# One line moved in an expert loop: a tile's result ahead of the split of the next w2

## The chip, the cores and the metric

The program runs on one core of a Trainium2 chip. The metric is the device time of one execution in microseconds (us); a smaller time is better. TensorE (PE) multiplies matrices, VectorE (DVE), ScalarE (ACT) and GpSimd (POOL) work on elements, and SyncE (SP) issues most of the transfers. Each engine takes its own list of instructions in order, and semaphores order the engines among each other.

## The reference

Three layers follow one another. A chunked attention gives 4608 rows of 512 numbers. A layer of 8 experts follows: each row goes to one expert, the one with the largest logit. The last layer is a dense one with a swish.

```python
def _moe_ref(x, expert_emb, tau, w1, w2):
    ...
    expert_idx = np.argmax(logits, axis=1)
    ...
    for e in range(E):
        mask = expert_idx == e
        h = np.maximum(x[mask] @ w1[e], 0.0)
        out[mask] = gate_w[mask, None] * (h @ w2[e])

def _moe2_ref(x, w_in, w_out):
    h = x @ w_in
    g = h * (1.0 / (1.0 + np.exp(-1.702 * h)))
    return (g @ w_out).astype(np.float32)
```

In the expert layer w1 is 512 x 1024 and w2 is 1024 x 512 for each expert. The change lies in this layer.

## The kernel before, in words

The kernel has three stages. In the profiled execution attention and gating take the first 245 us, the expert stage runs to about 678 us, and the dense layer takes the rest. The order of the instructions on every engine is the order in which the code is written (`tc.manual_schedule()`).

**Tiles.** The rows are sorted by expert and cut into tiles of 128 rows of one expert; an expert with fewer rows left fills its last tile with others. Tiles 0 to 2 come before the loop; the loop of line 1354 takes tiles 3 to 38 (`NSURE` to `SURE - 1`).

**Two halves of a number.** Every float32 operand is held as two float16 parts, a high and a low one, and each product is three matmuls. Weights come from memory as float32 into a staging buffer (`stg` for w1, `stgB` for w2) and are split on the core by `w_split`: ScalarE writes the high part (line 793), VectorE the low part (line 798), in 4 pieces of 128 x 1024. The one copy on the core, `w1HL` and `w2HL`, is written over when the expert changes.

**A switch.** Which tile begins a new expert is known only at run time. `swap(i, which)` (line 843) therefore puts the split under `tc.If(flag[i] > 0)` (line 847), a branch that ScalarE and VectorE take or pass. Whoever uses the weight afterwards waits for both engines at this place, whether the branch was taken or passed. In the profiled execution the expert changes at tiles 8, 12, 19, 25, 28, 32 and 37. `load_next` then has SyncE issue the load of the expert after that into the staging buffer, under a branch of its own (line 837).

**A tile's work.** `mm1(i)` is the first product, 96 matmuls 128 x 128 (line 897) into PSUM; ScalarE (line 904) and VectorE (line 905) take it out as `hT`, the high and the low part. `mm2_part(i)` is the second product, 24 matmuls 128 x 512 (line 930), into a PSUM bank `py`, of which there are two. `mm2_evac(i)` is what this document calls the result of a tile: ScalarE sums the squares of a row (line 943), VectorE makes a scale of it in small steps (lines 944 to 953), ScalarE writes the scaled high part (`y`, line 956), VectorE the low part and a tail (lines 957 and 960), and SyncE stores `y` (line 968).

**One round of the loop.** Round i issues in this order, each engine seeing only its own part:

1. first product of tile i, its transfer out of PSUM (`hT`);
2. transfers for later tiles: the transposed rows of tile i + 2, and others;
3. `swap(i + 1, 1)`: the branch with the split of w1 for tile i + 1;
4. a step of `dec`: a piece of w_in or w_out of the last layer is converted (lines 1251 to 1258 on VectorE, 1154 and 1148 on ScalarE, the rest on GpSimd), in rounds 5 to 36, two steps in rounds 11 and 19;
5. second product of tile i - 1;
6. `swap(i, 2)`: the branch with the split of w2 for tile i;
7. the result of tile i - 1.

So on TensorE the products stand as first(i), second(i - 1), first(i + 1), second(i), and the second product of tile i is the first to use what step 6 of round i leaves in `w2HL`.

Of the kernel before, what the change touches and what calls it, by code (L numbers as in the profile page):

```python
# [34 lines left out]
def kernel(  # L35
# [732 lines left out]
    def reg(ap, engines, hi):  # L768
        return nc.values_load(ap, engines=engines, min_val=0, max_val=hi)
# [10 lines left out]
    def w_split(which, c, n, eng, st=stg):  # L780

        hlf, o = divmod(c * n, 2048)
        _, H_, L_ = WL[which]
        if which == 1 and n == 1024:
            k, f = slice(c % 2 * 2, c % 2 * 2 + 2), slice(c // 2 * 512, c // 2 * 512 + 512)
            H_, L_ = H_[:, k, f], L_[:, k, f]
            src = st[c % 2].rearrange("p (a f) -> p a f", a=2)[:, :, f]
        else:
            flat = slice(c * n, (c + 1) * n)
            H_ = H_.rearrange("p a f -> p (a f)")[:, flat]  # L790
            L_ = L_.rearrange("p a f -> p (a f)")[:, flat]
            src = st[hlf][:, o:o + n]
        nc.scalar.activation(out=H_, in_=src, func=AF.Copy, scale=2.0 ** W_EXP)
        if eng is nc.gpsimd:
            eng.tensor_tensor(out=src, in0=src, in1=w_pow.to_broadcast([128, n]), op=ALU.mult)
            eng.tensor_tensor(out=L_, in0=src, in1=H_, op=ALU.subtract)
        else:
            eng.scalar_tensor_tensor(
                out=L_, in0=src, scalar=2.0 ** W_EXP, in1=H_, op0=ALU.mult, op1=ALU.subtract
            )  # L800
# [29 lines left out]
    def load_next(i, which):  # L830

        if which == 1:
            nxt[i] = (
                reg(nf_i[0:1, i:i + 1], [ENG.SP], 1), reg(nx_i[0:1, i:i + 1], [ENG.SP], NE - 1)
            )
        fl, e = nxt[i]
        with tc.If(fl > 0):
            for hlf in range(2):
                w_load(e, which, hlf, stage[which])
# [3 lines left out]
    def swap(i, which):  # L843

        if which == 1:
            flag[i] = reg(fl_i[0:1, i:i + 1], [ENG.Activation, ENG.DVE], 1)
        with tc.If(flag[i] > 0):  # L847
            for c in range(4):
                w_split(which, c, 1024, nc.vector, stage[which])
        load_next(i, which)  # L850
# [18 lines left out]
    def fetch(i):  # L869
        xg = mo.tile([128, 2 * DM], F16, tag="xg", name="xg", bufs=2)  # L870
        src = xs[0:NPART * 128, :] if i < NSURE else xs[:, :]
        nc.gpsimd.indirect_dma_start(  # L872
            out=xg[:, :], out_offset=None, in_=src,
            in_offset=bass.IndirectOffsetOnAxis(ap=mt_t[i].bitcast(I32)[:, 1:2], axis=0),
        )
        xg_t[i] = xg

    def turn(i):
        xT = mo.tile([128, 2 * KD, 128], F16, tag="xTm", name="xTm", bufs=2)
        nc.sync.dma_start_transpose(xT, xg_t.pop(i))  # L880
        xTm_t[i] = xT
# [28 lines left out]
    def mm1(i):  # L910
        for q in range(4):
            mm1_part(i, q)
# [19 lines left out]
    def mm2_evac(i):  # L932
        hT_t.pop(i)
        p = py_t.pop(i)
        mt = mt_t.pop(i)
        y = mo.tile([128, YP], F16, tag="y", name="y", bufs=2)
        ysq = mo.tile([128, DM], F16, tag="ysq", name="ysq", bufs=1)
        s = mo.tile([128, 4], F32, tag="ys", name="ysc", bufs=2)
        si = s.bitcast(I32)
        c_i = mt.bitcast(I32)[:, 0:1]  # L940
        tail = y[:, 2 * DM:YP].bitcast(I32).rearrange("p (a two) -> p a two", two=2)
        n = (YP - 2 * DM) // 4
        nc.scalar.activation(out=ysq, in_=p, func=AF.Square, scale=2.0 ** -20, accum_out=s[:, 0:1])
        nc.vector.tensor_scalar(si[:, 3:4], c_i, EXP_BITS, None, op0=ALU.bitwise_and)
        nc.vector.tensor_copy(tail[:, :, 0], mt.bitcast(I32)[:, 1:2].to_broadcast([128, n]))
        nc.vector.tensor_scalar(s[:, 0:1], s[:, 0:1], Y_MIN * 2.0 ** -40, None, op0=ALU.max)
        nc.vector.tensor_scalar(
            si[:, 1:2], si[:, 0:1], 24, 23, op0=ALU.logical_shift_right, op1=ALU.logical_shift_left
        )
        nc.vector.tensor_scalar(  # L950
            si[:, 1:2], si[:, 1:2], -1.0, float((BIAS + Y_TOP - 20) << 23), op0=ALU.mult, op1=ALU.add
        )
        nc.vector.scalar_tensor_tensor(  # L953
            out=si[:, 2:3], in0=c_i, scalar=MAN_BITS, in1=si[:, 1:2], op0=ALU.bitwise_and, op1=ALU.bitwise_or
        )
        nc.scalar.activation(out=y[:, 0:DM], in_=p, func=AF.Copy, scale=s[:, 2:3])  # L956
        nc.vector.scalar_tensor_tensor(
            out=y[:, DM:2 * DM], in0=p, scalar=s[:, 2:3], in1=y[:, 0:DM], op0=ALU.mult, op1=ALU.subtract
        )
        nc.vector.scalar_tensor_tensor(  # L960
            out=tail[:, :, 1], in0=si[:, 3:4].to_broadcast([128, n]), scalar=float(BIAS << 23),
            in1=si[:, 1:2].to_broadcast([128, n]), op0=ALU.add, op1=ALU.subtract,
        )
        if i < NSURE:
            nc.sync.dma_start(out=ys[i * 128:(i + 1) * 128, :], in_=y)
        elif i < SURE:
            row = reg(idx_y[0:1, i:i + 1], [ENG.SP], NT)
            nc.sync.dma_start(out=ys[bass.ds(row, 128), :], in_=y)
        else:
            nc.gpsimd.indirect_dma_start(  # L970
                out=ys[:, :], out_offset=bass.IndirectOffsetOnAxis(ap=idx_y[:, i:i + 1], axis=0),
                in_=y[:, :], in_offset=None,
            )
# [161 lines left out]
    def big_load(b):  # L1135

        nc.sync.dma_start(
            out=raw_o[b % NRAW].rearrange("p f two -> p (f two)"),
            in_=block_of(b).rearrange("p f two -> p (f two)"),
        )  # L1140
# [213 lines left out]
    for i in range(NSURE, SURE):  # L1354
        mm1(i)
        if i + 2 < SURE:
            turn(i + 2)
        if i == NSURE:
            load_next(NSURE - 1, 2)
            for b in range(NRAW):  # L1360
                big_load(b)
        if i + 3 < SURE:
            fetch(i + 3)
        if i + 4 < SURE:
            find(i + 4)
        if i + 1 < SURE:
            swap(i + 1, 1)
        if NSURE + 2 <= i < LASTD:
            for _ in range(2 if i in (NSURE + 8, NSURE + 16) else 1):
                next(dec, None)  # L1370
        if i > NSURE:
            mm2_part(i - 1, 0, KF)
        if i == SURE - 1:
            scales_b(0)
            early = sums(0)
            for _ in range(2):
                next(early)
        swap(i, 2)
        if i > NSURE:
            mm2_evac(i - 1)  # L1380
        if i == SURE - 2:
            scales_a(0)
        if i == LASTD:
            next(dec, None)
            dec_stack.close()
            mlp = ctx.enter_context(tc.tile_pool(name="mlp", bufs=1))

            def prep(j):
                idc = mlp.tile([128, 4, 2], I32, tag="idc", name="idc", bufs=2)
                nc.sync.dma_start(  # L1390
                    out=idc,
                    in_=ys[j * 512:(j + 1) * 512, 2 * DM:2 * DM + 4].bitcast(I32).rearrange(
                        "(a p) c -> p a c", p=128
                    ),
                )
                yT = mlp.tile([128, 2 * KD, 512], F16, tag="yT", name="yT", bufs=1)
                for a in range(4):
                    nc.sync.dma_start_transpose(
                        yT[:, :, a * 128:(a + 1) * 128],
                        ys[j * 512 + a * 128:j * 512 + (a + 1) * 128, 0:2 * DM],  # L1400
                    )
                yT_t[j], id_t[j] = yT, idc

            ring = {}

            def load_w(j, n):
                ring[j, n] = mlp.tile([128, 2, KG * 128], F16, tag="ring", name="ring", bufs=NRING)
                o = PROD[n][0]
                nc.sync.dma_start(
                    out=ring[j, n], in_=wod[2 * o:2 * o + 2].rearrange("h p f -> p h f")  # L1410
                )

            op6 = mlp.tile([128, 4096], F16, name="op6")
            prep(0)
            for n in range(NRING):
                load_w(0, n)
# [316 lines left out]
```

## Time and profile before

| what | number |
|---|---|
| median of 3 runs | 1385.8 us (1385.78 to 1392.34) |
| profiled execution, its own time | 1381.04 us |
| its span, first to last instruction | 1379.3 us |
| mean granted clock of TensorE, as a share of full speed | 0.968 |
| busy over the span: PE | 1248.8 us (91%) |
| busy over the span: DVE | 1048.1 us (76%) |
| busy over the span: ACT | 723.7 us (52%) |
| low parts of w2 in the loop, DVE line 798 | 28 pieces, mean 1349 ns |

The profile is one execution, recorded on the core. Busy is the time in which an engine worked on an instruction; register, branch and semaphore instructions do not count. Matmuls overlap each other, so their ends are modelled. The rows of a timeline give the start, the duration, the engine, the source line, the operation, what is written and read, and in square brackets how long the engine was idle before and which work released it. A releaser written ACTq or DVEq is not an instruction that computes but the queue of that engine: there the branch of line 847.

### The profile page before, as it was taken

What the parts mean: (1) busy time and instruction counts of PE and PEld (TensorE: products, weight loads), DVE (VectorE), ACT (ScalarE), POOL (GpSimd) and SP (SyncE); (2) the same over time, 40 slices, a digit from 0 to 9 for tenths busy, and PEclk for the clock granted to TensorE, in tenths of its full rate; (3) what the DMA queues carried; (4) which work ended last, traced back from release to release, by engine and by line L of the source; (5) the groups of instructions that cost most, each with busy time, mean ns of one, the idle gap of its engine ahead of it and who ended that gap; (6) DMA issues with size and microseconds to landing.
All of it is one profiled execution on the core that took longest, in us unless ns stands there. A gap on an engine that the chain in (4) does not pass through costs nothing.

```text
span 1379.3 us, 35366 instructions
## 1 busy us (share of the span) xinstructions
PE 1248.8 (91%) x14098; PEld 1028.0 (75%) x14098; DVE 1048.1 (76%) x1897; ACT 723.7 (52%) x1288; POOL 737.6 (53%) x687
## 2 busy tenths in 40 slices
PE   6886666999899899899989999999999999999996
PEld 5665555676577576667678888888888888888885
DVE  3888788648887878886679696968787896969681
ACT  6986755235534445454454545545454645455452
POOL 1564544214533444453157575766767675757664
PEclk9998877999999999999999999999999999999998
DMA  9999986388675759986506253443526072634412
GB/s 202 232 182 185 172 161 155 99 225 238 192 179 164 204 143 270 277 240 161 154 3 192 84 154 123 123 153 85 192 33 223 22 205 71 157 120 123 153 62 92
DMA packets 225749, 213.97 MB, mean 155 GB/s; under 512 B 134104, under 2 KB 178648, under 8 KB 225568
## 3 DMA queue, kind: packets, MB, share of 16 engines
q1 hardware_dynamic: 211024, 184.51, 52.7%
q0 software_dynamic: 7152, 19.70, 4.4%
q10 hardware_dynamic: 7392, 7.36, 1.7%
q8 instruction: 112, 1.84, 0.6%
q14 instruction: 69, 0.57, 0.1%
HBM read 155.02 MB, written 36.85 MB: 139 GB/s over the span
## 4 chain that ended last, share of the span: by engine, by line
PE 33%; DVE 5%; issue 5%; ACT 4%; POOL 3%; POOLq 0%; ACTq 0%; DVEq 0%
PE pa L1441 8%; PE pd L1441 8%; PE pb L1441 8%; PE gb L1441 4%; PE pc L1441 4%; DVE zA L1296 3%; ACT zA L1465 1%; POOL w2HL L1303 1%; POOL out_dram L1588 1%; ACT stgB L1299 1%; ACT w1HL L1299 1%; DVE stgB L1296 0%; ACT hT L1583 0%; ACT op L1299 0%; DVE zC L1462 0%
## 5 line engine op out<-in xcount | busy, mean ns | idle before, releaser
L1441 PEld LDWEIGHTS <-wS 128*128 128x128 f16 x3024 | 296.5, 98 | 59.7 <-issue 21.6
L897 PEld LDWEIGHTS <-w1HL 128*128 128x128 f16 x3744 | 215.6, 99 | 21.9 <-ACTq L847 7.5
L897 PE MATMUL ph<-xTm,w1HL 128*128 128x128 f16 x3744 | 221.4, 221 | 9.7 <-ACTq L847 5.3
L930 PE MATMUL py<-w2HL,hT 128*128 128x512 f16 x936 | 214.8, 386 | 12.3 <-ACTq L847 3.8
L930 PEld LDWEIGHTS <-hT 128*128 128x128 f16 x936 | 91.3, 99 | 119.8 <-issue 22.1
L872 POOL DMA_INDIRECT xg<-xs,mt x39 | 40.1, 1029 | 148.0 <-DMA mt<-mtab 90.2
L1441 PEld LDWEIGHTS <-w2HL 128*128 128x128 f16 x864 | 84.5, 98 | 10.6
L1441 PEld LDWEIGHTS <-w1HL 128*128 128x128 f16 x864 | 84.6, 98 | 9.8
L956 ACT ACTIVATE y<-py,ysc 128x512 f16<-128x512 f32 x39 | 26.8, 687 | 114.5 <-DVE ysc L953 114.5
L416 POOL TENSOR_TENSOR x<-x,sx_all 128x512 f32<-128x512 f32 x33 | 34.2, 1037 | 98.0 <-DVE rd L386 46.3
L1296 DVE TENSOR_TENSOR zA<-zA 128x512 f32<-128x512 f32 x72 | 73.2, 1017 | 10.8 <-POOL w2HL L1303 9.5
L905 DVE SCALAR_TENSOR_TENSOR hT<-ph,hT 128x512 f16<-128x512 f32 x78 | 51.8, 685 | 32.2 <-ACT hT L904 32.2
L1465 ACT ACTIVATE zA<-zA 128x512 f32<-128x512 f32 x72 | 45.2, 629 | 57.8 <-DVE zA L1462 35.3
L1303 POOL TENSOR_TENSOR w1HL<-zA,w1HL 128x512 f16<-128x512 f32 x36 | 54.1, 1503 | 36.6 <-ACT w1HL L1299 36.6
L904 ACT ACTIVATE hT<-ph 128x512 f16<-128x512 f32 x78 | 44.8, 594 | 49.6 <-PE ph L897 49.5
L1149 POOL TENSOR_TENSOR wS<-d_f,wS 128x512 f16<-128x512 f32 x28 | 38.3, 1386 | 52.2 <-ACTq L847 27.5
L1441 PE MATMUL pd<-stg,wS 128*128 128x256 f16 x456 | 55.9, 276 | 3.5 <-ACT stgB L1299 3.5
L1588 POOL DMA_INDIRECT out_dram<-hT,idc x36 | 35.6, 988 | 35.6 <-ACT hT L1583 32.5
L311 ACT ACTIVATE kuT<-tp 64x512 f32<-64x512 f32 x72 | 45.1, 626 | 17.4 <-PE tp L306 16.4
L306 PE MATMUL tp<-identF,ku 128*128 128x128 f32 x144 | 25.8, 322 | 29.3 <-DMA ku<-in_k_dram 25.6
L1441 PE MATMUL pa<-stg,wS 128*128 128x256 f16 x432 | 51.6, 273 | 0.7 <-ACT stgB L1299 0.7
L340 DVE TENSOR_REDUCE mx<-sp 128x8 f32<-128x512 f32 x36 | 24.8, 688 | 35.7 <-PE sp L333 35.6
(370 smaller groups left out, 3151.2 us busy)
## 6 DMA issues: line engine op xcount, KB each, us to landing
ring<-wod SPq DMA_DIRECT2D x63, 1024.0 KB
stg<-in_moe_w_dram SPq DMA_DIRECT2D x14, 1024.0 KB
stgB<-in_moe_w_dram SPq DMA_DIRECT2D x14, 1024.0 KB
ys<-y SPq DMA_DIRECT2D x39, 258.0 KB
vt<-in_v_dram SPq DMA_DIRECT2D x64, 144.0 KB
xs<-xr SPq DMA_DIRECT2D x36, 256.0 KB
raw_o<-in_moe_w_in_dram SPq DMA_DIRECT2D x16, 512.0 KB
raw_o<-in_moe_w_out_dram SPq DMA_DIRECT2D x16, 512.0 KB
```

Of the source, the lines that this page charges most:

```text
L311: lambda r=r, p=p, dst=dst: nc.scalar.activation(out=dst[:, :, r], in_=p[r * 64:(r + 1) * 64], func=AF.Copy)
L872: nc.gpsimd.indirect_dma_start(out=xg[:, :], out_offset=None, in_=src, in_offset=bass.IndirectOffsetOnAxis(ap=mt_t[i].bitcast(I32)[:, 1:2] ...
L897: nc.tensor.matmul(p[:, f % 4], wt[:, c, fs], xT[:, a, :], start=(c == 0 and a == 0 and wt is w1H), stop=(c == KD - 1 and wt is w1L),)
L904: nc.scalar.activation(out=hi, in_=p, func=AF.Relu)
L905: nc.vector.scalar_tensor_tensor(out=lo, in0=p, scalar=0.0, in1=hi, op0=ALU.max, op1=ALU.subtract)
L930: nc.tensor.matmul(p, hT[:, a, :], wt[:, c, :], start=st, stop=sp)
L1149: nc.gpsimd.tensor_tensor(out=L_, in0=f, in1=H_, op=ALU.subtract)
L1296: nc.vector.tensor_tensor(out=o, in0=x, in1=p, op=op)
L1303: eng.tensor_tensor(out=lo, in0=x, in1=hi, op=ALU.subtract)
L1441: nc.tensor.matmul(dst, lhs(a, k, ab), rhs(b, k), start=first and ab == abs_[0] and k == 0 and m == 0, stop=(k == n - 1 and m == 2), skip_ ...
L1465: nc.scalar.activation(out=z, in_=z, func=AF.Sigmoid, scale=1.702 * 2.0 ** -G_EXP)
L1588: disjoint("out", nc.gpsimd.indirect_dma_start(out=out[:, :], out_offset=bass.IndirectOffsetOnAxis(ap=id_t[j][0][:, 2 * h + t, 0:1], axis= ...
```

## The change

The two statements of steps 6 and 7 change places: the result of tile i - 1 is now issued ahead of the branch with the split of w2 for tile i. Nothing else is different.

```diff
             early = sums(0)
             for _ in range(2):
                 next(early)
-        swap(i, 2)
         if i > NSURE:
             mm2_evac(i - 1)
+        swap(i, 2)
         if i == SURE - 2:
             scales_a(0)
```

**VectorE.** The rows are of one round of the loop. L847 is the branch, L798 are the pieces of w2 in it, L944 to L960 are the result, L905 is the next tile's `hT`. Before:

```order
L847 COMPARE_AND_BRANCH
L798 SCALAR_TENSOR_TENSOR w2HL<-stgB_4652,w2HL 128x1024 x2
L798 SCALAR_TENSOR_TENSOR w2HL<-stgB_4653,w2HL 128x1024 x2
L847 UNCONDITIONAL_BRANCH x2
L837 UNCONDITIONAL_BRANCH
L944 TENSOR_SCALAR ysc<-mt 128x1
L945 COPY y<-mt 128x2
L946 TENSOR_SCALAR ysc<-ysc 128x1
L947 TENSOR_SCALAR ysc<-ysc 128x1
L950 TENSOR_SCALAR ysc<-ysc 128x1
L953 SCALAR_TENSOR_TENSOR ysc<-mt,ysc 128x1
L957 SCALAR_TENSOR_TENSOR y<-py_5395,ysc,y 128x512
```

And now, from the last rows of the result on:

```order
L953 SCALAR_TENSOR_TENSOR ysc<-mt,ysc 128x1
L957 SCALAR_TENSOR_TENSOR y<-py_5395,ysc,y 128x512
L960 SCALAR_TENSOR_TENSOR y<-ysc 128x2
L847 COMPARE_AND_BRANCH
L798 SCALAR_TENSOR_TENSOR w2HL<-stgB_4652,w2HL 128x1024 x2
L798 SCALAR_TENSOR_TENSOR w2HL<-stgB_4653,w2HL 128x1024 x2
L847 UNCONDITIONAL_BRANCH x2
L837 UNCONDITIONAL_BRANCH
L905 SCALAR_TENSOR_TENSOR hT<-ph,hT 128x512 x2
```

The whole branch, taken or not, has moved from ahead of L944 to behind L960, in every round. ScalarE's list changes in the same way, with L793 for L798 and L943 and L956 for the result.

**SyncE.** The rows are of the end of one round and the start of the next. L837 is the branch with the loads of a later w2 (L775), L968 is the store of the result, L880 is the transpose of a later tile's rows. Before:

```order
L837 COMPARE_AND_BRANCH
L775 ISA
L775 DMA stgB_4652<-in_moe_w_dram 128x4x512
L775 ISA
L775 DMA stgB_4653<-in_moe_w_dram 128x4x512
L837 UNCONDITIONAL_BRANCH x2
L769 TENSOR_LOAD idx_y
L769 ISA x2
L968 ISA
L968 DMA ys<-y 128x1032
L880 DMA_TRANSPOSE xTm<-xg 128x8x128
```

And now:

```order
L769 TENSOR_LOAD idx_y
L769 ISA x2
L847 UNCONDITIONAL_BRANCH
L968 ISA
L968 DMA ys<-y 128x1032
L837 COMPARE_AND_BRANCH
L775 ISA
L775 DMA stgB_4652<-in_moe_w_dram 128x4x512
L775 ISA
L775 DMA stgB_4653<-in_moe_w_dram 128x4x512
L837 UNCONDITIONAL_BRANCH x2
L880 DMA_TRANSPOSE xTm<-xg 128x8x128
```

The store has moved ahead of the loads; the transpose stands behind both, as it did.

## Rows read from the trace of the kernel before

**Rows 1.** Windows: busy of each engine (x instructions), TensorE's granted clock, DMA share, GB/s; tiles 3 to 38.

```profile
278.70:678.50 399.80, 379.34 (x4133) 269.58 (x4131) 310.41 (x545) 190.30 (x324) 159.68 (x134) 0.98 0.75 207
```

**Rows 2.** Timeline of TensorE: second products of tiles 5 and 6, no switch near.

```profile
299.80 5.34 PE L930 MATMUL py<-w2HL,hT 128*128 128x512 f16 x24
...
310.33 5.34 PE L930 MATMUL py<-w2HL,hT 128*128 128x512 f16 x24
```

**Rows 3.** Timeline of VectorE: the last instruction of the result of tile 5.

```profile
308.11 0.15 DVE L960 SCALAR_TENSOR_TENSOR y<-ysc 128x2 int32<-128x2 int32 x1
```

**Rows 4.** Timeline of VectorE: last dec instruction of round 24, ahead of the branch.

```profile
518.43 0.69 DVE L1258 SCALAR_TENSOR_TENSOR fo<-raw_o,d_t 128x512 int32<-128x512 int32 x1
```

**Rows 5.** Timeline of TensorE: second products of tiles 24 and 11, neither a switch.

```profile
519.24 5.12 PE L930 MATMUL py<-w2HL,hT 128*128 128x512 f16 x23 [0.80 <-DVEq L847]
...
371.04 7.64 PE L930 MATMUL py<-w2HL,hT 128*128 128x512 f16 x23 [0.87 <-DVEq L847]
```

**Rows 6.** Timeline of VectorE: split of tile 8's w1, ends of the results of tiles 6 and 8.

```profile
312.44 4.71 DVE L798 SCALAR_TENSOR_TENSOR w1HL<-stg,w1HL 128x1024 f16<-128x1024 f32 x4 [0.58 <-ACT w1HL L793]
...
324.37 0.15 DVE L960 SCALAR_TENSOR_TENSOR y<-ysc 128x2 int32<-128x2 int32 x1
...
346.50 0.15 DVE L960 SCALAR_TENSOR_TENSOR y<-ysc 128x2 int32<-128x2 int32 x1
```

**Rows 7.** Timeline of TensorE: second products of tiles 7 and 9.

```profile
320.88 5.34 PE L930 MATMUL py<-w2HL,hT 128*128 128x512 f16 x24
...
345.28 5.34 PE L930 MATMUL py<-w2HL,hT 128*128 128x512 f16 x24
```

**Rows 8.** Timeline of VectorE: ends of the results of tiles 10, 13 and 17.

```profile
374.49 1.01 DVE L960 SCALAR_TENSOR_TENSOR y<-ysc 128x2 int32<-128x2 int32 x1
...
403.55 2.77 DVE L960 SCALAR_TENSOR_TENSOR y<-ysc 128x2 int32<-128x2 int32 x1
...
450.52 0.15 DVE L960 SCALAR_TENSOR_TENSOR y<-ysc 128x2 int32<-128x2 int32 x1
```

**Rows 9.** Timeline of TensorE: second products of tiles 14, 18 and 19.

```profile
404.96 5.34 PE L930 MATMUL py<-w2HL,hT 128*128 128x512 f16 x24
...
447.12 5.34 PE L930 MATMUL py<-w2HL,hT 128*128 128x512 f16 x24
...
462.93 7.78 PE L930 MATMUL py<-w2HL,hT 128*128 128x512 f16 x23 [2.56 <-DVE w2HL L798]
```

**Rows 10.** Timeline of VectorE: ends of results 23 and 24, between them tile 25's w2.

```profile
522.78 0.15 DVE L960 SCALAR_TENSOR_TENSOR y<-ysc 128x2 int32<-128x2 int32 x1
...
527.10 4.62 DVE L798 SCALAR_TENSOR_TENSOR w2HL<-stgB,w2HL 128x1024 f16<-128x1024 f32 x4
...
533.91 0.15 DVE L960 SCALAR_TENSOR_TENSOR y<-ysc 128x2 int32<-128x2 int32 x1
```

**Rows 11.** Timeline of TensorE: first product of tile 30, second of 31, first of 34.

```profile
572.31 5.42 PE L897 MATMUL ph<-xTm,w1HL 128*128 128x128 f16 x94 [0.81 <-DVEq L847]
...
599.33 5.34 PE L930 MATMUL py<-w2HL,hT 128*128 128x512 f16 x24
...
618.03 7.05 PE L897 MATMUL ph<-xTm,w1HL 128*128 128x128 f16 x94 [0.80 <-DVEq L847]
```

**Rows 12.** Timeline of VectorE: ends of the results of tiles 30 and 37.

```profile
601.77 0.15 DVE L960 SCALAR_TENSOR_TENSOR y<-ysc 128x2 int32<-128x2 int32 x1
...
676.26 0.15 DVE L960 SCALAR_TENSOR_TENSOR y<-ysc 128x2 int32<-128x2 int32 x1
```

**Rows 13.** Timeline of TensorE: second product of tile 38, and the dense layer's first wait.

```profile
673.37 5.34 PE L930 MATMUL py<-w2HL,hT 128*128 128x512 f16 x24 [0.73 <-ACTq L847]
...
683.71 2.72 PE L1441 MATMUL pd<-stg,wS 128*128 128x256 f16 x12 [2.38 <-ACT stgB L1299]
```

**Rows 14.** Waits, 250 to 690 us: who waited for whom, us in total, times, longest.

```profile
PE ph L897 <- ACTq L847: 5.3, 4, 1.7
...
PE ph L897 <- DVEq L847: 3.5, 6, 0.8
```

## Prediction

> **What bounds the kernel now.** I read the page for the three stages, then the windows, then the timelines of TensorE and VectorE side by side for each switch of expert, last the waits. In the expert loop TensorE is busy 379.34 of 399.80 us [rows 1]: it is the bound, and about 20 us of waits can move. VectorE, 310.41 us busy, has room on average; the question is where it runs late.
>
> A tile without a switch near shows the room. The second product of tile 5 starts at 299.80 and ends at 305.14; VectorE ends that tile's result at 308.11 + 0.15 = 308.26, so 3.12 us behind it [rows 2, 3]. The second product of tile 6 starts at 310.33. The result is ready 2.07 us before that.
>
> Whether this matters hangs on the branch. Tile 24 is no switch, so its branch is passed; still, 23 of its 24 matmuls wait 0.80 us for VectorE's queue at line 847 and start at 519.24, which is 0.12 us after VectorE's last dec instruction, 518.43 + 0.69 = 519.12 [rows 4, 5]. Tile 11 waits in the same way [rows 5]. So **a passed branch holds the second product as well**, until ScalarE and VectorE have done everything listed ahead of it.
>
> **The change part by part.** No instruction is added or removed. In each round the branch moves behind the result, and the second product of tile i may now start only 0.12 us after VectorE's end of the result of tile i - 1. That is a new wait. Behind the branch on VectorE and ScalarE are the next tile's `hT` and the next split; for the branch itself TensorE waits.
>
> *Rounds in step.* The room of 2.07 us covers it: no cost. The cover is gone where VectorE is over 1.95 us late, and that is around switches: it has four pieces of w1, a dec step, the result, then four pieces of w2.
>
> *How lateness carries over.* From a split of w1 until it has caught up, VectorE has no wait for TensorE, so a TensorE that stands still does not make it later, and an early wait can take the place of one that came after the split. I therefore count, for each switch, by how much the last place where TensorE waits for VectorE moves. At a switch VectorE does the same work in another order, plus a bubble: before, ScalarE had the high parts of w2 ready ahead of VectorE; now ScalarE starts them behind `y`. The trace of before has no such bubble. Its bounds are 0 (VectorE still has line 957 to do meanwhile) and the 0.58 us that VectorE waited at the start of a w1 split [rows 6]; I take 0.4.
>
> *Tiles 7 to 9.* VectorE ends the result of tile 6 at 324.52, while tile 7's product starts at 320.88 [rows 6, 7]: now it waits 3.76 us. At tile 9 VectorE ends the result of tile 8 at 346.65; with 0.4 and 0.12 that is 347.17 against 345.28 [rows 6, 7]. **+1.9**, the rest being swallowed.
>
> *Tile 11 (w1 of tile 12, two dec steps).* The result of tile 10 ends at 374.49 + 1.01 = 375.50 [rows 8], with 1.9 carried and 0.12: 377.5 against 371.04 [rows 5], 6.5 in all. **+4.6.** TensorE runs slowly after this wait already: 7.64 us for 23 matmuls, against 5.12 at tile 24 [rows 5]. I take that as unchanged.
>
> *Tile 14.* The result of tile 13 ends at 403.55 + 2.77 = 406.32, because one small instruction took 2.77 us instead of 0.15; the product starts at 404.96 [rows 8, 9]. **+1.5** if that comes again, 0 if not. I keep it, since line 960 was also long at tile 10 [rows 8].
>
> *Tiles 18 and 19.* Tile 18: 450.67 + 0.12 against 447.12, a wait of 3.67 [rows 8, 9]. Tile 19: its split starts behind the result, some 2.4 us of VectorE's time (from 527.10 + 4.62 to 534.06 it is 2.34 [rows 10]), plus the bubble. The 23 matmuls start 2.8 us later than at 462.93, and before they took 7.78 us [rows 9]. If they run at full rate now, 2.7 us of this comes back and 0.1 is left; if not, 2.8. **+1.5**, the middle, since the wait at tile 18 may take the slow stretch on itself.
>
> *Tiles 24 to 28.* Tile 24: 522.93 + 0.12 = 523.05 instead of 519.24 [rows 5, 10]. Here the new wait feeds back: the product ends at 528.17, its result 3.12 later at 531.29, then 0.4, then the split of 4.62: 536.31, where before split and result were done at 534.06 [rows 10]. VectorE is 2.25 us later, and stays so through the split of tile 28's w1, since it has no room there; tile 28's split adds 0.4. The first product of tile 30 waits for VectorE before and after [rows 11]. **+2.65.**
>
> *Tiles 31 to 34.* Tile 31: 601.92 + 0.12 against 599.33, a wait of 2.7, swallowed because tile 34's first product waits for VectorE until 618.03 anyway [rows 11, 12]; what is left is 0.4. But 94 matmuls there took 7.05 us, against 5.42 at tile 30 after the same wait [rows 11]. If TensorE is not slowed this time, 1.6 comes back. With half of it: **-0.4**, ends -1.2 and +0.4.
>
> *Tiles 37 and 38.* By then dec is done and VectorE is in step; I count the bubble, 0.4. Tile 38's product has to wait until 676.41 + 0.12 instead of starting at 673.37, 3.16 us; the dense layer then waits 2.38 us for ScalarE, whose list doesn't hang on that product [rows 12, 13], and takes that much up. **+1.2.**
>
> *The other queues.* SyncE issues the store and the loads in the other order, the transpose still behind both; at a switch the three end with VectorE's split as before. GpSimd's list of work is the same. Nothing there.
>
> Sum: 1.9 + 4.6 + 1.5 + 1.5 + 2.65 - 0.4 + 1.2 = 12.95, say **13 us**. The profiled execution (1381.04 with 1379.3 of span) would take 1394.0. It lies 4.8 under the median of the three runs, so I add to the median: 1385.8 + 13 = 1398.8, **1399 us**, or 0.9% more. The ends of the terms give +8 (0 at tile 14, 0.1, -1.2, 0.4 at the end) to +18 (2.8 at tile 19, slow matmuls at tile 24 as well, nothing swallowed at the end).
>
> **The clock, row and rule.** Behind long waits rows show TensorE slower: matmuls of tiles 11, 19 and 34 [rows 5, 9, 11]. At tile 30 a wait of the same kind left the rate as it was [rows 11]. The Trainium skill, "TensorE: Matmul & The Clock Gate", section "HAM oscillation — how this bites in real kernels", says that waits between groups of matmuls put the engine back to the lower clock each time, so that each next group starts cold. By that rule each of the longer new waits would be paid twice. The trace agrees at three places and not at tile 30, hence a rival and not the forecast.
>
> **The rivals.**
>
> *More slow stretches.* The new waits at tiles 7, 18, 24 and 31 (3.76, 3.67, 3.8 and 2.7 us) each cost a slow stretch of 7.64 - 5.12 = 2.5 us more [rows 5], and none is swallowed: 13 + 10 = 23, so 1409. For it: three waits did this. Against it: a slow TensorE next to a late VectorE costs little, and tile 30.
>
> *Waits change places.* The lateness at tiles 11 and 24 is swallowed as well, as at tile 7, and only the bubbles stay: 7 x 0.4 = 2.8, so 1388.6. It would be so if VectorE reached the result of tile 10 earlier than the row says, for instance if its long instructions are collisions that don't come again. Against it: 6.5 us at tile 11 is far more than such a collision.
>
> *The earlier result pays.* With the result first, ScalarE's `y` no longer waits behind the split, and VectorE gets to the `hT` behind the split earlier. Then the first products' waits for the branch, 5.3 + 3.5 = 8.8 us [rows 14], go: 1377.0, faster. It decides by whether VectorE's end of `hT` after a split is earlier than now by more than the new waits. Against it: VectorE does the same work, and waits for `y` either way.
>
> That the change doesn't do what it says can be ruled out: the rows of the order show the branch behind the result.
>
> **How the numbers follow.** Chances: forecast 0.60 (1394 to 1404), slow stretches 0.20, places changed 0.15, faster 0.05. About 0.5%, 6.9 us, is what a measurement can tell from no change. Slower by more than that: 0.60 + 0.20 = 0.80; within it 0.15; faster 0.05. The range reaches from under 1388.6 to above 1409: 1387 to 1410.
>
> **What would show it.** Right: second products of tiles 7, 11, 18, 24, 27 and 31 that start 0.1 us after VectorE's line 960 and wait for the queue at line 847; second products in step, tiles 5 or 16, unchanged; the dense layer as long as before; the loss between 310 and 680 us. The carrying over is wrong if the delay of tile 9 is near 3.8 and not 1.9; the clock if matmuls of tiles 7 or 18 take over 7 us. The whole is wrong if passed branches don't hold the second product: then tile 7 starts right behind the first product of tile 8.

## The result, and the profile after

The changed kernel takes 1406.18 us, median of 4 runs (1402.57 to 1408.14), against 1386.82 for 4 runs of the kernel before on the same chip (1385.78 to 1392.34): **1.0112 [1.0078, 1.0145], slower by about 1.1%**. By that ratio it is 15.5 us; the medians lie 19.4 apart. A second session gave 1402.67 against 1390.47, 1.0106 [1.0071, 1.0142]. The forecast was 1399, slower, with 1394 to 1404 as its own band.

The profiled execution took 1402.57 us with a span of 1400.8, which is 21.5 us more than the span before. Not all of that is the change's. From the second product of tile 3, the first one in the loop, to the first matmul into `pa`, a PSUM bank of the dense layer, it is 433.29 us, before 415.96: **17.3 us**. From there to the end it is 684.51 against 684.62. The other 4.3 us lie ahead of that product, and this piece varies by itself: it began at 277.33 us in one profile of the new order and at 292.25 in one of an old order.

Windows of the changed kernel (columns as in [rows 1]): the whole stage, then the stretches around the second products of tiles 7, 11, 18 and 30.

```profile
283.03:703.60 420.57, 386.45 (x4134) 269.92 (x4130) 308.38 (x549) 193.96 (x327) 164.76 (x135) 0.96 0.72 198
326.00:338.00 12.00, 9.57 (x72) 5.40 (x72) 9.14 (x17) 5.12 (x10) 8.73 (x7) 0.86 0.79 239
379.00:390.00 11.00, 9.00 (x42) 3.94 (x42) 6.50 (x11) 4.16 (x8) 5.68 (x6) 0.65 0.52 150
459.00:468.00 9.00, 7.55 (x34) 3.29 (x34) 7.74 (x11) 4.83 (x9) 6.21 (x6) 0.81 0.68 209
606.00:614.00 8.00, 7.51 (x64) 4.51 (x64) 7.85 (x8) 6.41 (x10) 7.06 (x5) 1.00 0.71 157
```

To the dense layer's first matmul, into the bank `pd`, the stage has grown from 399.80 us [rows 1] to 420.57, and TensorE is busy 386.45 of it, before 379.34. So 7.1 us of the growth are matmuls that ran longer, and the other 13.7 are waits. 3.4 us come back right behind the stage, between `pd` and `pa`; 2.38 of them are the wait in `pd` [rows 13], which is gone. The granted clock, as a mean of the stretch, fell to between 0.65 and 0.86 of full speed at tiles 7, 11 and 18; behind the wait at tile 30 it stayed at 1.00.

Timeline of TensorE after. The second products, in order, are those of tiles 5 [answering to rows 2], 7 and 9 [rows 7], 11 [rows 5], 14 and 18 [rows 9], 24 [rows 5], 27, 30 and 31 [rows 11], 35 and 38 [rows 13]; the L897 row is the first product of tile 35.

```profile
304.21 5.34 PE L930 MATMUL py<-w2HL,hT 128*128 128x512 f16 x24
...
327.94 0.38 PE L930 MATMUL py<-w2HL,hT 128*128 128x512 f16 x1 [1.96 <-ACTq L847]
328.81 6.69 PE L930 MATMUL py<-w2HL,hT 128*128 128x512 f16 x23 [0.49 <-DVEq L847]
...
351.23 5.34 PE L930 MATMUL py<-w2HL,hT 128*128 128x512 f16 x24
...
379.86 0.58 PE L930 MATMUL py<-w2HL,hT 128*128 128x512 f16 x1 [7.38 <-ACTq L847]
381.58 7.60 PE L930 MATMUL py<-w2HL,hT 128*128 128x512 f16 x23 [1.14 <-DVEq L847]
...
416.38 5.12 PE L930 MATMUL py<-w2HL,hT 128*128 128x512 f16 x23 [0.54 <-DVEq L847]
...
459.96 0.38 PE L930 MATMUL py<-w2HL,hT 128*128 128x512 f16 x1 [1.48 <-ACTq L847]
460.83 6.81 PE L930 MATMUL py<-w2HL,hT 128*128 128x512 f16 x23 [0.49 <-DVEq L847]
...
534.37 6.32 PE L930 MATMUL py<-w2HL,hT 128*128 128x512 f16 x23 [0.30 <-DVEq L847]
...
570.60 6.81 PE L930 MATMUL py<-w2HL,hT 128*128 128x512 f16 x23 [0.49 <-DVEq L847]
...
606.83 5.12 PE L930 MATMUL py<-w2HL,hT 128*128 128x512 f16 x23 [0.49 <-DVEq L847]
...
618.82 0.38 PE L930 MATMUL py<-w2HL,hT 128*128 128x512 f16 x1 [1.50 <-ACTq L847]
619.68 5.12 PE L930 MATMUL py<-w2HL,hT 128*128 128x512 f16 x23 [0.49 <-DVEq L847]
...
648.37 5.52 PE L897 MATMUL ph<-xTm,w1HL 128*128 128x128 f16 x96 [1.73 <-DMA xTm<-xg]
...
666.64 5.12 PE L930 MATMUL py<-w2HL,hT 128*128 128x512 f16 x23 [0.49 <-DVEq L847]
...
696.95 6.81 PE L930 MATMUL py<-w2HL,hT 128*128 128x512 f16 x23 [0.49 <-DVEq L847]
```

Tile 5 runs in step, as before. From tile 7 on, the second products of ten tiles that are no switch wait for the queue at line 847. Which instruction they wait for is in the timeline of VectorE after: ends of the results of tiles 6 [rows 6], 7 (with the split of tile 8's w2 behind it), 10 and 13 [rows 8], 17 [rows 8], 23 [rows 10] and 34.

```profile
328.55 0.15 DVE L960 SCALAR_TENSOR_TENSOR y<-ysc 128x2 int32<-128x2 int32 x1
...
338.95 0.15 DVE L960 SCALAR_TENSOR_TENSOR y<-ysc 128x2 int32<-128x2 int32 x1
339.22 4.63 DVE L798 SCALAR_TENSOR_TENSOR w2HL<-stgB,w2HL 128x1024 f16<-128x1024 f32 x4
...
380.46 1.01 DVE L960 SCALAR_TENSOR_TENSOR y<-ysc 128x2 int32<-128x2 int32 x1
...
413.81 2.45 DVE L960 SCALAR_TENSOR_TENSOR y<-ysc 128x2 int32<-128x2 int32 x1
...
460.57 0.15 DVE L960 SCALAR_TENSOR_TENSOR y<-ysc 128x2 int32<-128x2 int32 x1
...
534.08 0.17 DVE L960 SCALAR_TENSOR_TENSOR y<-ysc 128x2 int32<-128x2 int32 x1
...
666.38 0.15 DVE L960 SCALAR_TENSOR_TENSOR y<-ysc 128x2 int32<-128x2 int32 x1
```

328.55 + 0.15 = 328.70, and the 23 matmuls start at 328.81; 381.47 and 381.58; 416.26 and 416.38; 460.72 and 460.83; 534.25 and 534.37; 666.53 and 666.64. The lag is 0.11 or 0.12 us each time, and the same at the other four tiles (27, 30, 31 and 38). In the kernel before, these 23 matmuls of tiles 7, 11, 18 and 24 started 3.4, 4.5, 3.3 and 3.7 us ahead of the end of that result.

Waits of the changed kernel, 250 to 710 us (columns as in [rows 14]), and in the second fence those of second products before, 250 to 690 us:

```profile
PE py L930 <- ACTq L847: 22.6, 9, 7.4
...
PE py L930 <- DVEq L847: 5.4, 10, 1.1
...
PE ph L897 <- ACTq L847: 0.9, 1, 0.9
...
PE ph L897 <- DVEq L847: 0.7, 2, 0.4
```

```profile
PE py L930 <- ACTq L847: 3.8, 2, 3.1
...
PE py L930 <- DVEq L847: 2.7, 3, 1.0
```

The first products' waits of [rows 14] have shrunk from 8.8 us to 1.6, and these lie ahead of tile 3's second product. In their place second products wait 28.0 us at the branch; before it was 6.5. ScalarE waits less for VectorE's scale (78.0 us, before 114.5) and more for second products (86.7 us, before 45.5).

### The profile page after: what moved, and what is told of

The parts are those of the page before. It is cut to its first block, busy times and chain, and to the rows that moved or that the text cites. A ratio compares the mean times of both kernels' runs of the same rounds, so it can differ in the third digit from the quotient of the medians.

```text
span 1400.8 us, 35376 instructions
## 1 busy us (share of the span) xinstructions
PE 1261.0 (90%) x14098; PEld 1032.0 (74%) x14098; DVE 1042.5 (74%) x1897; ACT 726.6 (52%) x1288; POOL 742.3 (53%) x687
## 5 line engine op out<-in xcount | busy, mean ns | idle before, releaser
L930 PE MATMUL py<-w2HL,hT 128*128 128x512 f16 x936 | 223.2, 394 | 31.4 <-ACTq L847 22.6
L897 PEld LDWEIGHTS <-w1HL 128*128 128x128 f16 x3744 | 215.1, 99 | 19.2 <-issue 5.3
L897 PE MATMUL ph<-xTm,w1HL 128*128 128x128 f16 x3744 | 221.4, 221 | 6.8 <-issue 2.5
L1441 PEld LDWEIGHTS <-w2HL 128*128 128x128 f16 x864 | 84.5, 98 | 10.6
L905 DVE SCALAR_TENSOR_TENSOR hT<-ph,hT 128x512 f16<-128x512 f32 x78 | 52.2, 688 | 42.1 <-ACT hT L904 39.1
L943 ACT ACTIVATE ysq<-py 128x512 f16<-128x512 f32 x39 | 23.2, 594 | 93.0 <-PE py L930 86.7
L956 ACT ACTIVATE y<-py,ysc 128x512 f16<-128x512 f32 x39 | 26.8, 687 | 81.0 <-DVE ysc L953 78.0
```

The source lines that it names most:

```text
L897: nc.tensor.matmul(p[:, f % 4], wt[:, c, fs], xT[:, a, :], start=(c == 0 and a == 0 and wt is w1H), stop=(c == KD - 1 and wt is w1L),)
L905: nc.vector.scalar_tensor_tensor(out=lo, in0=p, scalar=0.0, in1=hi, op0=ALU.max, op1=ALU.subtract)
L930: nc.tensor.matmul(p, hT[:, a, :], wt[:, c, :], start=st, stop=sp)
L1441: nc.tensor.matmul(dst, lhs(a, k, ab), rhs(b, k), start=first and ab == abs_[0] and k == 0 and m == 0, stop=(k == n - 1 and m == 2), skip_ ...
```

## The experiments

The new order does two things at once. In rounds without a switch the passed branch now stands behind the result (theory A, **the held branch**: the prediction's). In the seven rounds with a switch the split itself now starts behind the result, so the new expert's first second product gets its weight later (theory B, **the late split**). Rivals are SyncE's order, and the lower clock behind the new waits. Delays below tell how much later than in the kernel before a tile's second product runs, taken at its second matmul, since the first one is often released by itself; both kernels are counted from the start of tile 3's second product. In the changed kernel the delay is 1.6 us at tile 9, 6.2 at 12, 7.4 at 20, 12.6 at 29, 12.1 at 33, 16.1 at 37, and 17.3 at `pa`.

### The two halves apart

The new order only in the rounds that hold a split, as a diff to the changed kernel:

```diff
-        if i > NSURE:
+        if i in (8, 12, 19, 25, 28, 32, 37):
             mm2_evac(i - 1)
-        swap(i, 2)
+            swap(i, 2)
+        else:
+            swap(i, 2)
+            if i > NSURE:
+                mm2_evac(i - 1)
```

> The new order only in the seven rounds whose tile begins a new expert (8, 12, 19, 25, 28, 32, 37), the old order in all others. Held branch (the branch, passed as well, holds the second product until the result ahead of it is done, where VectorE is late): 0 to +5 us against before, and second products of tiles 7, 11, 24, 27 and 31 start as before. Late split (the split of w2 itself starts later and holds the new expert's first second product): nearly all of the loss, +12 to +19 us. SyncE (the store ahead of the loads delays later transfers; loads are issued in these rounds alone): also nearly all, +12 to +19 us.

1389.18 us, **1.0047 [1.0022, 1.0073]**, 6.5 us over before by the ratio; the stage to `pa` is 10.6 us longer in the profile. Timeline of TensorE of this kernel, second product of tile 8:

```profile
336.53 0.43 PE L930 MATMUL py<-w2HL,hT 128*128 128x512 f16 x1 [3.35 <-ACT w2HL L793]
337.79 7.95 PE L930 MATMUL py<-w2HL,hT 128*128 128x512 f16 x23 [0.82 <-DVE w2HL L798]
```

The waits are for the split weight itself; tile 19 waits in the same way, 6.40 + 0.67 us. VectorE's split of tile 8's w2 started at 336.51, behind a result that ended at 336.24 + 0.15 = 336.39. In the kernel before it started at 330.68, and this profile's loop begins 1.4 us later: 4.4 us, which is the delay of tile 8, 4.45. The delay is 4.3 us at tile 9, 6.9 at 20, 11.5 at 33. Theory A alone had given this kernel nearly nothing, and theory B had given it more than it shows: the late split is real, and is not the whole.

The new order only in the rounds just ahead of these, where the branch is passed:

```diff
-        if i > NSURE:
+        if i in (7, 11, 18, 24, 27, 31, 36):
             mm2_evac(i - 1)
-        swap(i, 2)
+            swap(i, 2)
+        else:
+            swap(i, 2)
+            if i > NSURE:
+                mm2_evac(i - 1)
```

> The new order only in the seven rounds before those (7, 11, 18, 24, 27, 31, 36), in which w1 is split and the branch for w2 is passed. Held branch: +8 to +16 us, and the second products of tiles 7, 11, 18, 24, 27 and 31 start 0.1 us after the result of the tile before. Late split and SyncE: 0 to +2 us, since no w2 is split or loaded in these rounds.

1384.59 us, **1.0021 [0.9997, 1.0044]**, 2.9 us over before; the stage is 5.1 us longer. Timeline of TensorE, second product of tile 7:

```profile
325.82 0.38 PE L930 MATMUL py<-w2HL,hT 128*128 128x512 f16 x1 [1.96 <-ACTq L847]
326.68 6.61 PE L930 MATMUL py<-w2HL,hT 128*128 128x512 f16 x23 [0.49 <-DVEq L847]
```

The same waits as in the changed kernel (there 1.96 + 0.49 us), but most of them are given back: the delay is 3.3 us at tile 7 and 1.5 at 9, 8.1 at 18 and 4.2 at 20, 8.3 at 27 and 6.0 at 29, 9.2 at 32 and 4.7 from 33 on. With the split at its old place, the wait behind the switch shrinks by what was waited ahead of it. My expectation of +8 or more for this half fell.

At tile 37 the halves' delays, 11.5 and 4.7, add up to the 16.1 of the changed kernel. By the ratios they add up to less (6.5 + 2.9 = 9.4 us, the whole 15.5), with intervals that overlap, and 4.0 us of the changed kernel's delay arose at tiles 34 and 35, where neither half shows any. So the shares are rough here; the next two kernels give them again.

### No passed branch at all

The program then branches only where this input has a switch, in the new order and in the old one; what is left out are the branches on w2 in all other rounds, so these two kernels fit this input alone. In the new order:

```diff
         if i > NSURE:
             mm2_evac(i - 1)
-        swap(i, 2)
+        if i in (8, 12, 19, 25, 28, 32, 37):
+            swap(i, 2)
+        else:
+            load_next(i, 2)
```

> The new order in all rounds, and the branch with the split of w2 only in the seven rounds that take it; rounds that would pass it have none (for these inputs nothing else changes). Held branch: the loss is gone, and with it the waits that the kernel before has at tiles 11, 24 and 27 for a passed branch: -10 to +3 us against before. Late split: +12 to +19 us as with the whole change. SyncE: +12 to +19 us as well.

1384.39 us, **1.0024 [0.9997, 1.0051]**: most of the loss is gone. In the old order, the same replacement ahead of the result:

> The order of before, and the branch with the split of w2 only in the seven rounds that take it. With the changed order and no passed branch it was 1.0024 of before. If the two parts of the loss add (a passed branch behind the result, and a split behind the result): without passed branches the old order is faster than before by what passed branches cost there, -1 to -6 us, and the changed order without them lies 5 to 10 us above this kernel. If the position of the split costs nothing without the passed branches: this kernel is +1 to +5 us against before, as the changed order without them was.

1385.43 us against 1390.47 for before in that session, **0.9968 [0.9949, 0.9988]**. So without passed branches the new order is 1.0024 / 0.9968 = 1.0056 of the old one, 7.8 us (3 to 12 with the two intervals taken together): that is the late split by itself, near the 6.5 of the first experiment. In the profiles of the two kernels the stage is 417.93 and 411.31 us, 6.6 apart. With passed branches the new order is 1.0112, 15.5 us, so the held branch is the other 7.7. **By the ratios the late split is 6.5 to 7.8 us of the loss, and the held branch 2.9 by itself and 7.7 beside the late split.** By the profiles it is 6.6 to 10.6 and 5.1 to 10.7 of 17.3. That both take part is shown, the late split by an interval clear of 1 and the held branch by its rows; which is the larger is not. (The passed branches cost the old order something too, 4.4 us by the ratio and 4.7 in the stage.) Timeline of TensorE, new order without passed branches, around tile 12:

```profile
379.31 0.39 PE L897 MATMUL ph<-xTm,w1HL 128*128 128x128 f16 x2 [3.27 <-ACTq L847]
381.26 7.24 PE L897 MATMUL ph<-xTm,w1HL 128*128 128x128 f16 x94 [1.55 <-DVEq L847]
```

Tile 11's wait of 7.38 + 1.14 us is gone, and its delay is -3.7; at tile 12 it is +1.0, because the first product of tile 13, shown here, waits for the same VectorE. **A wait that is removed comes back at the next place where TensorE meets VectorE**, as long as VectorE's own list has not got shorter: here 8.52 us at tile 11 came back as 4.82 at the next product.

### SyncE's order

The result ahead of the branch on the computing engines, but its store behind the branch and the loads on SyncE:

```diff
         if i > NSURE:
-            mm2_evac(i - 1)
+            mm2_evac(i - 1, False)
         swap(i, 2)
+        if i > NSURE:
+            y_store(i - 1)
```

> The new order on VectorE and ScalarE in all rounds, but SyncE's store of the result behind the loads of the next w2, as before. Held branch and late split: the loss stays, +12 to +20 us. SyncE: the loss goes, 0 to +5 us.

1397.22 us, **1.0107 [1.0058, 1.0156]**: the loss stays whole. The order of store and loads is not the cause.

### The clock

The changed kernel with matmuls that nobody reads, put ahead of second products so that TensorE has something to do while it waits:

```diff
+        for _ in range({7: 30, 11: 110, 18: 25, 19: 30, 24: 54, 27: 30}.get(i - 1, 0)):
+            nc.tensor.matmul(gb[:, 0:128], ones16, ones16, start=True, stop=True)
         if i > NSURE:
             mm2_part(i - 1, 0, KF)
```

> The changed kernel with matmuls that nobody reads (128 x 128, into an unused bank) ahead of the second products of tiles 7, 11, 18, 19, 24 and 27, so many that they fill about three quarters of the waits there. Clock: a good part of the loss is slow matmuls behind these waits; 3 to 8 us less than the changed kernel, so +8 to +13 us against before, with second products of full rate there. Waits alone: no gain, +13 to +18 us.

1401.03 us, **1.0073 [1.0042, 1.0104]** (the changed kernel: 1.0112 and 1.0106). The stage is 9.4 us longer than before, not 17.3, and the delay at tile 37 is 8.9, not 16.1. Timeline of TensorE, tile 18; then windows of the whole stage, of this kernel and of the one with the store last (columns as in [rows 1]).

```profile
461.26 1.56 PE L1372 MATMUL gb<-ones 128*128 128x128 f16 x25
...
463.77 5.12 PE L930 MATMUL py<-w2HL,hT 128*128 128x512 f16 x23 [0.49 <-DVEq L847]
```

```profile
289.54:702.88 413.34, 393.98 (x4412) 283.76 (x4410) 311.80 (x549) 193.87 (x327) 162.57 (x135) 0.99 0.74 201
...
277.33:701.24 423.91, 385.80 (x4132) 270.93 (x4130) 307.78 (x549) 193.64 (x327) 160.33 (x135) 0.96 0.72 196
```

Tile 18's product still starts 0.11 us behind VectorE, but its 23 matmuls take 5.12 us instead of 6.81. That tile alone proves little: in the kernel with the store last, without these matmuls, it waited 1.42 + 0.49 us and took 5.12 too. The whole stage says more. The granted clock was 0.98 before, 0.96 in the changed kernel, in its second profile and with the store last, and 0.99 here. So **the lower clock behind the waits is about 5 us of the loss by the ratios (0.0033 to 0.0039 of 1390), 7 to 8 by the profiles**. The intervals of the ratios overlap; it is the rows of the stage that show it. The rest is the waits themselves. No run was made to tell whether the held or the late kind of wait lowers the clock. In the one profile of each half, TensorE is busy 385.03 us of the stage at 0.96 with the late split alone, and 379.32 at 0.97 with the passed branches alone, against 379.34 before [rows 1]: the added slow time came with the late split there.

### Where dec stands

Around a switch VectorE is late because it has a split, a dec step and a result in a row. Four kernels move dec. The first puts it between the branch and the result, in the old order (branch, dec, result), as a diff to the kernel before:

```diff
-        if NSURE + 2 <= i < LASTD:
-            for _ in range(2 if i in (NSURE + 8, NSURE + 16) else 1):
-                next(dec, None)
...
         swap(i, 2)
+        if NSURE + 2 <= i < LASTD:
+            for _ in range(2 if i in (NSURE + 8, NSURE + 16) else 1):
+                next(dec, None)
         if i > NSURE:
             mm2_evac(i - 1)
```

> The order of before, but the dec step behind the branch and ahead of the result (branch, dec step, result). Revised theory, VectorE's chain: around a switch TensorE waits for whatever VectorE has ahead of the branch, and the dec steps are part of that; without them ahead of it, the waits of before at tiles 11, 19, 24 and 27 shrink, some of it coming back at the next first product: -3 to -10 us against before. If dec steps are hidden anyway: within 3 us of before.

1387.49 us, 0.9968 [0.9942, 0.9993]: faster by a hair. Repeated with more runs:

> The order branch, dec step, result once more, with more rounds: -2 to -8 us against before if the first measurement (0.9968) holds; within 2 us if it was chance.

1389.85 us, **0.9996 [0.9978, 1.0013]**: the gain did not come again in the time, so this order by itself shows no change beyond the noise. (In both profiles the stage to `pa` is 4.0 us shorter than before, 411.91 and 411.94 against 415.96, so a small gain is not excluded.) The second and third put dec last, behind the result and the branch in the new order, and behind the branch and the result in the old. In the new order:

```diff
-        if NSURE + 2 <= i < LASTD:
-            for _ in range(2 if i in (NSURE + 8, NSURE + 16) else 1):
-                next(dec, None)
...
         swap(i, 2)
+        if NSURE + 2 <= i < LASTD:
+            for _ in range(2 if i in (NSURE + 8, NSURE + 16) else 1):
+                next(dec, None)
```

> The changed order with the dec step last (result, branch, dec step). VectorE's chain: most of the loss of the change was the dec step, the result and the split standing in a row ahead of the second product; without the dec step the result is done about when the second product could start: -8 to +3 us against before. If the loss comes from the result ahead of the split alone: +8 to +16 us.

1400.03 us, **1.0065 [1.0042, 1.0088]**. I had expected the loss to go. Timeline of TensorE, first products of tiles 10 and 13, behind the switches at 8 and 12:

```profile
355.13 7.05 PE L897 MATMUL ph<-xTm,w1HL 128*128 128x128 f16 x94 [3.42 <-DVEq L847]
...
392.42 7.05 PE L897 MATMUL ph<-xTm,w1HL 128*128 128x128 f16 x94 [1.40 <-DVEq L847]
```

Now dec stands ahead of the branch that the next first product waits for, and the wait has moved there, with the slow matmuls. In the old order, the same lines moved behind `mm2_evac`:

> The order of before with the dec step last (branch, result, dec step). VectorE's chain: -3 to -10 us, as with the dec step between, a little worse where VectorE then idles ahead of the result. If dec steps are hidden anyway: within 3 us.

1393.93 us, 1.0011 [0.9989, 1.0032], no change; the gain that I had expected did not come. The fourth keeps the order branch, dec, result, and takes the two double dec steps out of rounds 11 and 19, which touch the switches at 12 and 19, into rounds 14 and 22:

```diff
-            for _ in range(2 if i in (NSURE + 8, NSURE + 16) else 1):
+            for _ in range(2 if i in (NSURE + 11, NSURE + 19) else 1):
                 next(dec, None)
```

> As the one before, and the two rounds with two dec steps are rounds 14 and 22 instead of 11 and 19, which stand at switches for these inputs. VectorE's chain: the first products of tiles 13 and 20 wait less (4.9 and 5.8 us there, with slow matmuls behind): -8 to -16 us against before. If these waits come from ScalarE's or GpSimd's part of other work: as without it, -2 to -8 us.

1378.63 us (1374.34 to 1381.82), **0.9919 [0.9893, 0.9944]**: faster than before, by 0.8%, and than the changed kernel, by 24 us. Timeline of TensorE: the longest wait behind the switch at 12, here at the first product of tile 14, and, in the second fence, in the kernel with the same order and the old rounds (the repeat above), at the first product of tile 13.

```profile
393.39 0.28 PE L897 MATMUL ph<-xTm,w1HL 128*128 128x128 f16 x2 [1.18 <-ACTq L847]
394.49 5.42 PE L897 MATMUL ph<-xTm,w1HL 128*128 128x128 f16 x94 [0.81 <-DVEq L847]
```

```profile
387.18 0.28 PE L897 MATMUL ph<-xTm,w1HL 128*128 128x128 f16 x2 [3.37 <-ACTq L847]
389.12 7.02 PE L897 MATMUL ph<-xTm,w1HL 128*128 128x128 f16 x94 [1.66 <-DVEq L847]
```

5.03 us of wait have become 1.99, and the 94 matmuls take 5.42 us instead of 7.02. The stage is 407.23 us, against 411.94 with the old rounds. Behind the switch at 19 a wait of 5.06 + 0.70 us became 1.06 + 0.81. The double steps cost this much because of where they stood. Their new rounds suit the switches of this input; with other rows the switches fall elsewhere. The order of the kernel before with the double steps moved was not run.

The changed kernel was run once more beside these:

> The changed kernel once more, next to the others: +12 to +19 us (1.0112 the first time), with the second products of tiles 7, 11, 14, 18, 24, 27 and 31 0.11 us behind the result of the tile before, and two to five slow stretches more than before in the expert loop.

1402.67 us, 1.0106 [1.0071, 1.0142], as told above.

## Why the prediction was right, and where not

The sign and the place held, and so did the mechanism that it named, as one of two: a forecast of +13 us, and 15.5 by the ratio or 17.3 in the stage. That the sum came so near is in part luck. The measured 1406.18 lies inside the range but outside the band of the forecast, nearer to the rival's 1409 than to 1399 (the ratio's 15.5 is nearer to 13), and terms that were too high (tiles 14, 18 to 20) offset terms that were too low or missing (24 to 29, 34 and 35). The upper end of the sum, with the slow matmuls at the 2.5 us of the rival, would have been 19 and not 18. The terms, as growth of the delay in the profile:

| tiles | forecast | measured |
|---|---|---|
| 7 to 9 | +1.9 | +1.6 |
| 10 to 13 | +4.6 | +4.6 |
| 14 | +1.5 | +0.7 |
| 18 to 20 | +1.5 | +0.5 |
| 21 to 23 | none | +0.1 |
| 24 to 29 | +2.65 | +5.1 |
| 30 to 33 | -0.4 | -0.5 (+1.6 at 30, -2.1 to 33) |
| 34, 35 | none | +4.0 |
| 36 to `pa` | +1.2 | +1.2 |

**"A passed branch holds the second product as well"** was right, to 0.12 us at every tile that was named.

**"How lateness carries over"** was right: tile 7 is 3.39 us late and tile 9 only 1.63; the half with passed branches alone shows the same.

**"SyncE ... at a switch the three end with VectorE's split as before. ... Nothing there"** was the step that failed at tiles 34 and 35. The split of tile 32's w2 is itself later, and the loads wait for it. Timeline of SyncE before, the transpose, and in the second fence after:

```profile
617.34 2.38 SPq L880 DMA_TRANSPOSE xTm<-xg  x1
```

```profile
631.98 3.18 SPq L775 DMA_DIRECT2D stgB<-in_moe_w_dram  x2
635.46 5.21 SPq L880 DMA_TRANSPOSE xTm<-xg  x1
```

The transpose is issued 18.12 us later; 4.33 of that lie ahead of tile 3's second product, and tile 33's delay is 12.05. 18.12 - 4.33 - 12.05 = 1.74, about the wait of 1.73 in tile 35's first product. That the rows had come just in time before is not shown: with the late split alone 12.48 us from this issue to that product were enough, and before there were 12.76. Behind it the result of tile 34 comes late, and the product of tile 35 has to wait for it. Timeline of ScalarE after:

```profile
663.51 0.60 ACT L943 ACTIVATE ysq<-py 128x512 f16<-128x512 f32 x1 [3.77 <-POOL sg L1149]
```

Tile 34's product had ended at 653.72 + 5.34 = 659.06, but ScalarE took it up at 663.51, held by GpSimd's part of dec. Before the change a result held in this way held no product. I had looked for late results at VectorE's long instructions and not at this round. Why the kernel with the store last has the same two waits (delays of 14.8 at tile 33, 18.8 at 34 and 19.8 at 35), as has the second profile of the changed kernel, and neither half has them was not settled.

**"More slow stretches"**, the rival, came in part, and is about what tiles 24 to 29 cost beyond the forecast: the slow matmuls at tiles 24 and 27 are 6.32 + 6.81 - 2 x 5.12 = 2.9 us, and 5.1 - 2.65 = 2.45. Tiles 7 and 18 were slow too (6.69 and 6.81), by 1.6 to 1.7 us each and not the 2.5 that I had taken from tile 11; there most of it was swallowed. The sign for the clock, over 7 us at tiles 7 or 18, was set too high: it would have missed them. The Trainium skill, "TensorE: Matmul & The Clock Gate", section "HAM oscillation — how this bites in real kernels", tells of a kernel in which the waits between groups of matmuls put the engine back to the lower clock each time. The rows agree at tiles 7, 11, 18, 24, 27 and 38, and not at 14, 30, 31 and 35.

**"Plus a bubble", 0.4**, was too much: the result of tile 7 ends at 339.10 and the split starts at 339.22, and at no switch is it over 0.13 us. What I called a bubble hid a larger thing: at a switch the split stands behind the whole result, and the first experiment shows 4.3 us for it behind tile 8 alone. The sum came out near all the same, since I counted by the last wait of each switch, which holds both; the reason given, the held branch, is only a part of it, 2.9 to 7.7 us of 15.5 by the ratios.

**"The earlier result pays"** was right in its first half: of the 8.8 us of waits in [rows 14] 1.6 are left. The second products' waits grew by 21.5 us instead.

## What to carry to other kernels

In this program a branch that decides whether a buffer is rewritten also orders the engines when it is passed: whoever uses the buffer afterwards waits for everything listed ahead of the branch, on every engine that has it, at ten tiles to 0.11 or 0.12 us. So work that the user doesn't need goes behind such a branch, and the rewrite itself as early as its operands allow. Where an engine is late only around rare events, look first at what optional work stands beside those events: moving two dec steps gained more (0.9919) than any order within the round did (0.9996).

## What the runs showed that I had not expected

- Two waits of one length left TensorE at different rates. At tile 18 it waited 1.48 + 0.49 us and the 23 matmuls took 6.81; at tile 31 it waited 1.50 + 0.49 and they took 5.12. With the store last tile 18 waited 1.42 + 0.49 us and took 5.12. A slow group cannot be forecast from the wait ahead of it alone.
- Matmuls that nobody reads paid: with 279 of them added, the stage was 7.9 us shorter than the changed kernel's (425.39 us to `pa`, against 433.29).
- VectorE's long small instruction came again at the same place: line 960 of tile 13 took 2.77 us before [rows 8] and 2.45 after, of tile 10 1.01 in both, against 0.15 as a rule. It is hardly chance: at tile 13 it ended 0.02 us behind a pair of subtractions of dec that GpSimd ran beside it, and at tile 10 0.03 us behind one, which ended at 375.47. That this is the cause was not tried by a run. Timeline of GpSimd at tile 13, before, and in the second fence after:

```profile
403.81 2.49 POOL L1157 TENSOR_TENSOR d_f<-d_f 128x512 f32<-128x512 f32 x2
```

```profile
413.74 2.50 POOL L1157 TENSOR_TENSOR d_f<-d_f 128x512 f32<-128x512 f32 x2
```

- A first answer of 0.9968 with an interval clear of 1 became 0.9996 on repetition, with the same kernel and more runs.
